# Two one-column constants in one SBUF tile: every tile allocated after them lies 32 bytes lower

## The chip, the core and the metric

The kernel runs on one core of one Trainium2 chip. The core has a matrix engine (TensorE, PE in the profile, with PEld for its weight loads), a vector engine (VectorE, DVE), a scalar engine (ScalarE, ACT), a general engine (GpSimd, POOL) and a queue that issues transfers (SyncE, SP). They share an on-chip memory, SBUF, of 128 partitions; matmul results go to a second memory, PSUM. The metric is the device time of one execution in microseconds, as the median of repeated runs.

## What is computed

The reference has two parts. The first works on `x`, 8 batches of 3008 rows by 256 features, in float32:

```
X  = rfft(x, axis=1)                       # over the 3008 rows
Yr = Xr @ w_r - Xi @ w_i + b_r
Yi = Xr @ w_i + Xi @ w_r + b_i
Yr, Yi = sign(Y) * maximum(abs(Y) - 0.01, 0)   # each of the two
y  = irfft(Yr + 1j * Yi, n=3008, axis=1)
```

The second is a feed-forward layer over all 24,064 rows of `y`, with `w_in` of 256 by 2048 and `w_out` of 2048 by 256 in float64:

```
h = y @ w_in
g = h - tanh(h)
out = g @ w_out
```

## The kernel before

**The transforms.** 3008 is 64 times 47, so a transform is done in two matrix steps, first over the 47 and then over the 64. `Forward` loads pieces of `x` (tile `xt`), splits each into a high and a low float32r part (`x_h`, `x_l`) and multiplies by the constants `f1_h`, `f1_l`; the result goes through `st` to a buffer `a` in HBM. `Spectrum` reads it back transposed (`at`), does the second step against the constant `f2`, the complex linear layer (`cross`, `shared`, line 274), the threshold, and the first inverse step (`inverse`), and stores `zo` to a buffer `z`. `Chunk.load` reads that back as `zin`.

**The feed-forward layer.** The rows are cut into 52 chunks: 50 of 470 columns and two of 282. `Chunk.time` does the last inverse step against the constant `i2` and leaves `yh`, `yl`. For each of 16 slices of the 2048 hidden units, `up` runs six matmuls into `h` (line 410), ScalarE takes the tanh (`th`, line 413), VectorE subtracts (`g`, line 415), ScalarE rounds (`gh`, line 417), VectorE takes the remainder (`gl`, line 423), and `down` runs six matmuls into the two accumulators `o` (line 435). Float64 weights are turned into `win_h`, `win_l`, `wout_h`, `wout_l` at the start by integer operations (`split_f64`).

**Order.** The order on every engine is the order in which the code is written (`manual_schedule`). The first batch goes through a path of its own (`WholeSpectrum`), before any chunk can run; the later batches' transforms are put between the feed-forward steps by a table of slots. `up` runs two steps ahead of `down`.

**Placement.** Pools take their SBUF space in the order of their tiles, each tile rounded up to a multiple of 32 bytes per partition. The pool `const` comes first, and its first tiles are the four weight tiles, 16,384 bytes each; then come `below` and `rebias`, of one float32 column each, then `f1_h` and all the rest, and after `const` the pools `load`, `work`, `cvt` and `ffn`. The slots in them are multiples of 64 bytes long; shared slots of the `ffn` pool are 2,048 bytes.

**The two constants.** `below` holds -0.01 and is the bias of the threshold's activations (lines 351 and 357). `rebias` holds -896 and is the bias of the activation that shifts the exponent in the weight conversion (line 165).

**Where a read starts.** `f2` has 384 columns; the second forward step for frequency j reads four runs of 32 columns from it, which begin `m0[j]` columns into each of its four blocks of 96 columns. `m0` comes out of `index_maps`. By its formula, the unit with j = 6 and 7 has m0 = 56 and 55, and the unit with j = 12 and 13 has m0 = 48 and 47.

Of the kernel before, what the change touches and what calls it, by code (L numbers as in the profile page):

```python
# [10 lines left out]
F32 = mybir.dt.float32  # L11
# [55 lines left out]
def spectral_ffn(ctx, tc, x, w_r, w_i, b_r, b_i, w_in, w_out, f1, f2, i1, i2, out):  # L67
    nc = tc.nc
    P = 128
# [7 lines left out]
    const = ctx.enter_context(tc.tile_pool(name="const", bufs=1))  # L77
# [410 lines left out]
    with tc.manual_schedule(engines={E.PE, E.Activation, E.DVE, E.Pool, E.SP}):  # L488
# [5 lines left out]
        def idle(n):  # L494
            ps = ps_h.tile([P, 512], F32, name="idle", tag="h")
            for _ in range(n):
                nc.tensor.matmul(ps, warm[:, :P], warm, start=True, stop=True)

        idle(11)
        below = const.tile([P, 1], F32, name="below")  # L500
        nc.vector.memset(below, -LAM)
        rebias = const.tile([P, 1], F32, name="rebias")
        nc.vector.memset(rebias, -896.0)
        f1h, f1l = split(load_whole(f1, [94, 96], "f1", tag="tmp", bufs=4), "f1")
        first = [Forward(0, ch) for ch in range(NP // XC)]
# [179 lines left out]
```

## Time and profile before

| what | value |
|---|---|
| median of 3 runs | 2722.16 us (2720.28 to 2723.64) |
| the profiled execution | 2724.98 us |
| its span from the first to the last instruction | 2723.2 us |
| mean granted TensorE clock | 0.997 |
| PE busy | 2708.1 us, 99% |
| DVE, ACT busy | 1745.8 us (64%), 1383.1 us (51%) |
| DMA queue of the kernel | 104,960 packets, 161.13 MB, 19.8% of 16 engines |

The span is what the trace covers; 1.8 us of the profiled execution's time lie outside of it. Busy time of an engine is the time in which at least one of its instructions ran. "Idle before" is the idle time of an engine just ahead of an instruction, with what ended it. Line numbers (L435) are those of the kernel before.

### The profile page before, as it was taken

Reading aid. Unit: us, or ns where it says so; the run is one execution under the profiler, and the core shown is the slowest. Engines: PE = TensorE matmul, PEld = TensorE weight load, DVE = VectorE, ACT = ScalarE, POOL = GpSimd, SP = SyncE. Lnnn points to the kernel's source line nnn. Section 1 sums busy time; section 2 is a strip of 40 time slices with the busy share of each in tenths; the row PEclk is TensorE's granted clock in tenths of the full one; section 3 lists DMA queues with packets and bytes.
Section 4 is the critical chain, followed back from the end, with each engine's and each line's share of the span. In section 5 each row is a group of like instructions: output and inputs, shape, how many; then the busy total and the mean of one; then the engine's idle time right before and its main releaser. Section 6 shows DMA issues by size and latency. Waiting matters only on the chain.

```text
span 2723.2 us, 36979 instructions
## 1 busy us (share of the span) xinstructions
PE 2708.1 (99%) x14181; PEld 2401.2 (88%) x14181; DVE 1745.8 (64%) x3077; ACT 1383.1 (51%) x2589; POOL 1.5 (0%) x5
## 2 busy tenths in 40 slices
PE   9999999999999999999999999999999999999999
PEld 6788988999889998899988999899988999888889
DVE  6796786666556666566755667666665666555555
ACT  5556455454554446454455445644455445444444
POOL 0000000000000000000000000000000000000000
PEclk8999999999999999999999999999999999999999
DMA  6413223110231103111022110411113111000000
GB/s 195 134 61 111 74 85 108 46 53 25 65 93 40 52 32 109 56 47 46 24 79 80 46 46 31 117 55 49 38 43 106 45 38 43 33 22 22 22 17 16
DMA packets 105135, 163.47 MB, mean 60 GB/s; under 512 B 7488, under 2 KB 70976, under 8 KB 104864
## 3 DMA queue, kind: packets, MB, share of 16 engines
q1 hardware_dynamic: 104960, 161.13, 19.8%
q8 instruction: 111, 1.82, 0.3%
q14 instruction: 64, 0.52, 0.1%
HBM read 86.13 MB, written 74.97 MB: 59 GB/s over the span
## 4 chain that ended last, share of the span: by engine, by line
PE 98%; DMA 1%; DVE 1%; ACT 0%; issue 0%; SPq 0%; ACTq 0%; DVEq 0%
PE o L435 38%; PE h L410 38%; PE ps_v L274 4%; PE ps_i L397 4%; PE ps_f L254 3%; PE ps_t L274 2%; PE ps_f L205 1%; PE ps_f L206 1%; PE ps_f L207 1%; PE ps_v L342 1%; PE ps_i L309 1%; PE ps_i L310 1%; PE ps_i L311 1%; DMA xt<-in_x 0%; PE ps_i L365 0%; PE ps_t L342 0%
## 5 line engine op out<-in xcount | busy, mean ns | idle before, releaser
L415 DVE TENSOR_TENSOR g<-h,th 128x470 f32<-128x470 f32 (+1 forms) x832 | 531.7, 639 | 563.1 <-ACT th L413 559.3
L413 ACT ACTIVATE th<-h 128x470 f32<-128x470 f32 (+1 forms) x832 | 463.6, 557 | 783.1 <-PE h L410 780.5
L423 DVE TENSOR_TENSOR gl<-g,gh 128x470 fp32r<-128x470 f32 (+1 forms) x832 | 531.0, 638 | 286.9 <-ACT gh L417 205.5
L417 ACT CAST gh<-g 128x470 fp32r<-128x470 f32 (+1 forms) x832 | 483.5, 581 | 403.1 <-DVE g L415 393.2
L435 PE MATMUL o<-gh,wout_l 128*128 128x470 f32 (+1 forms) x1664 | 632.1, 380 | 1.1 <-ACT gh L417 1.1
L435 PE MATMUL o<-gl,wout_h 128*128 128x470 f32 (+1 forms) x1664 | 620.1, 373 | 0.7 <-DVE gl L423 0.7
L435 PE MATMUL o<-gh,wout_h 128*128 128x470 f32 (+1 forms) x1664 | 619.8, 372 | 0.0
L410 PE MATMUL h<-yl,win_h 128*128 128x470 f32 (+1 forms) x1664 | 485.5, 373 | 0.0
L410 PE MATMUL h<-yh,win_l 128*128 128x470 f32 (+1 forms) x1664 | 484.9, 372 | 0.0
L410 PE MATMUL h<-yh,win_h 128*128 128x470 f32 (+1 forms) x1664 | 484.5, 372 | 0.0
L435 PEld LDWEIGHTS o<-gl,wout_h 128*128 128x128 f32 x1664 | 313.2, 188 | 41.2 <-DVE gl L423 1.1
L410 PEld LDWEIGHTS h<-yh,win_l 128*128 128x128 f32 x1664 | 311.5, 188 | 41.0 <-ACT yh L401 0.4
L410 PEld LDWEIGHTS h<-yl,win_h 128*128 128x128 f32 x1664 | 311.4, 188 | 40.2
L435 PEld LDWEIGHTS o<-gh,wout_l 128*128 128x128 f32 x1664 | 313.8, 189 | 37.4 <-ACT gh L417 1.6
L410 PEld LDWEIGHTS h<-yh,win_h 128*128 128x128 f32 x1664 | 311.4, 188 | 40.0
L435 PEld LDWEIGHTS o<-gh,wout_h 128*128 128x128 f32 x1664 | 313.3, 188 | 34.0
L299 DVE TENSOR_TENSOR y<-tb,ps_v 64x256 f32<-64x256 f32 x384 | 160.1, 417 | 11.9 <-ACT tb L346 6.6
L397 PEld LDWEIGHTS ps_i<-i,zin 96*128 96x128 f32 x1024 | 126.1, 192 | 4.0 <-issue 0.5
L397 PE MATMUL ps_i<-i,zin 96*128 96x94 f32 x1024 | 127.8, 272 | 0.1
L91 DVE TENSOR_TENSOR x_l<-xt,x_h 94x512 fp32r<-94x512 f32 x128 | 86.8, 686 | 50.1 <-ACT x_h L90 48.7
L254 PEld LDWEIGHTS ps_f<-f,at 128*128 128x128 f32 x768 | 101.1, 191 | 10.2 <-issue 4.4
L254 PE MATMUL ps_f<-f,at 128*128 128x128 f32 x768 | 102.6, 276 | 1.9 <-DMA at<-a 1.9
(96 smaller groups left out, 2087.4 us busy)
## 6 DMA issues: line engine op xcount, KB each, us to landing
xt<-in_x SPq DMA_DIRECT2D x64, 384.0 KB, 3.6
at<-a SPq DMA_DIRECT2D x96, 256.0 KB, 2.8
z<-zo SPq DMA_DIRECT2D x96, 256.0 KB, 2.0
out<-ot SPq DMA_DIRECT2D x50, 470.0 KB, 2.9
a<-st SPq DMA_DIRECT2D x56, 384.0 KB, 3.2
zin<-z SPq DMA_DIRECT2D x44, 480.0 KB, 4.3
w_raw<-in_moe_w_in SPq DMA_DIRECT2D x8, 512.0 KB, 5.7
w_raw<-in_moe_w_out SPq DMA_DIRECT2D x8, 512.0 KB, 4.9
```

The lines of the kernel that those rows point to most:

```text
L91: rest.tensor_tensor(out=lo, in0=src, in1=hi.bitcast(F32), op=ALU.subtract)
L205: nc.tensor.matmul(pv, f1h, xl, start=True, stop=False)
L254: nc.tensor.matmul(pv[:, t, jj], self.at[:, jj, t * P:(t + 1) * P], rhs, start=True, stop=True)
L274: nc.tensor.matmul(dst, lhs[:, t], rhs[:, t, :], start=n == 0, stop=n == 5)
L299: nc.vector.tensor_tensor(out=y[ri * 64:(ri + 1) * 64, jj, :], in0=common(jj, ri), in1=self.vv[jj * 64:(jj + 1) * 64, ri * D:(ri + 1) * D] ...
L397: nc.tensor.matmul(ps[:, k * 94:(k + 1) * 94], self.zt[:, k, t * P:(t + 1) * P], i2t[:, p * 94:(p + 1) * 94], start=True, stop=True,)
L410: nc.tensor.matmul(h[:, :n], lhs[:, t, f * P:(f + 1) * P], rhs[:, t, :n], start=k == 0, stop=k == 5)
L413: nc.scalar.activation(out=th[:, :n], in_=h[:, :n], func=AF.Tanh)
L415: nc.vector.tensor_tensor(out=g[:, :n], in0=h[:, :n], in1=th[:, :n], op=ALU.subtract)
L417: nc.scalar.copy(out=gh[:, :n], in_=g[:, :n])
L423: nc.vector.tensor_tensor(out=gl[:, :n], in0=g[:, :n], in1=gh[:, :n].bitcast(F32), op=ALU.subtract)
L435: nc.tensor.matmul(self.o[t][:, :n], lhs[:, f, t * P:(t + 1) * P], rhs[:, :n], start=f == 0 and k == 0, stop=f == NF - 1 and k == 2,)
```

## The change

One tile `shifts` of two columns takes the place of the two tiles of one column, and `below` and `rebias` become its columns 0 and 1:

```diff
         idle(11)
-        below = const.tile([P, 1], F32, name="below")
+        shifts = const.tile([P, 2], F32, name="shifts")
+        below, rebias = shifts[:, 0:1], shifts[:, 1:2]
         nc.vector.memset(below, -LAM)
-        rebias = const.tile([P, 1], F32, name="rebias")
         nc.vector.memset(rebias, -896.0)
```

The start addresses in a partition, in bytes, as the two built programs have them:

| tile | before | after |
|---|---|---|
| `win_h`, `win_l`, `wout_h`, `wout_l` | 16512, 32896, 49280, 65664 | the same |
| `below` | 82048 | 82048 |
| `rebias` | 82080 | 82052 |
| `f1_h` | 82112 | 82080 |
| `f2` | 84928 | 84896 |
| `i2` | 88000 | 87968 |
| first `xt` | 112320 | 112288 |
| first `yh` | 145088 | 145056 |
| first `gl`, `gh`, `th`, `g` | 204480, 210624, 216768, 222912 | 204448, 210592, 216736, 222880 |

Before, all tiles from `f1_h` on start at a multiple of 64 bytes (192 past a multiple of 256 for nearly all of them); after, they start 32 past a multiple of 64 (160 past a multiple of 256). The four weight tiles start at a multiple of 64 in both.

The order on VectorE at the start of the program, the difference of after from before; `zero` and `warm` feed the filler matmuls, and `f_l` is the low part of `f1`:

```order
 L490 MEMSET zero 128x512
 L492 CAST warm<-zero 128x512
-L501 MEMSET below 128x1
-L503 MEMSET rebias 128x1
+L502 MEMSET shifts 128x1
+L503 MEMSET shifts 128x1
 L91 TENSOR_TENSOR f_l<-f_f,f_h 94x96
```

The two memsets stay two and stand where they stood. On every engine and queue all instructions stand in the same order in both programs, and each waits for the same semaphore values; only addresses differ, in 16,418 of the operands that matmuls read and in nearly all operands of VectorE, ScalarE and the transfers.

## The prediction

> **What bounds the kernel now.** I read the page's head and its chain of work first, then the busy times by stage, then what TensorE waited for, then single matmuls in the timeline. These are the head, the engines' busy time and the chain:
>
> ```profile
> span 2723.2 us, 36979 instructions
> ...
> PE 2708.1 (99%) x14181; PEld 2401.2 (88%) x14181; DVE 1745.8 (64%) x3077; ACT 1383.1 (51%) x2589; POOL 1.5 (0%) x5
> ...
> PE 98%; DMA 1%; DVE 1%; ACT 0%; issue 0%; SPq 0%; ACTq 0%; DVEq 0%
> ```
>
> TensorE carries 98% of the chain. The table by stage cuts the span where the work changes: the first batch's forward step, its spectrum, the stretch with weight conversion, the steady stretch, and the end:
>
> ```profile
> 0.00:34.00 34.00, 27.81 (x94) 18.96 (x95) 17.07 (x32) 16.98 (x31) 1.49 (x5) 0.90 0.83 236
> 34.00:110.00 76.00, 72.84 (x314) 55.21 (x312) 55.09 (x116) 40.32 (x73) 0.00 (x0) 0.93 0.47 145
> 110.00:450.00 340.00, 338.20 (x1775) 297.07 (x1774) 258.51 (x459) 192.36 (x367) 0.00 (x0) 1.00 0.32 96
> 450.00:2400.00 1950.00, 1949.79 (x10301) 1741.19 (x10301) 1245.84 (x2186) 982.37 (x1834) 0.00 (x0) 1.00 0.18 54
> 2400.00:2723.20 323.20, 319.48 (x1705) 288.77 (x1703) 169.33 (x285) 151.06 (x285) 0.00 (x0) 1.00 0.06 21
> ```
>
> The columns are the stretch, its length, then busy time of PE, PEld, DVE, ACT and POOL, the granted clock, the DMA share and GB/s. From 450 to 2400 us TensorE is idle for 0.21 of 1950 us, at a full clock. So there the time is the number of matmuls by their spacing, and nothing else. Only before 110 us do other engines and transfers reach the end: PE is idle 6.19 + 3.16 us there, and the clock is at 0.90 and 0.93. What TensorE waited for at the start and in the two feed-forward products:
>
> ```profile
> PE idle L497 <- DVE rebias L503: 1.9, 1, 1.9
> ...
> PE o L435 <- ACT gh L417: 1.1, 1, 1.1
> PE o L435 <- DVE gl L423: 0.7, 1, 0.7
> ```
>
> Total, times and longest: the 9,984 matmuls of lines 410 and 435 were kept waiting twice, for 1.8 us together.
>
> **The change, part by part.** Nothing is added, removed or moved in the order: two memsets stay two, every wait stays. So each term is the price of the same instruction at another address.
>
> *The memsets and the constants.* The two memsets and their place:
>
> ```profile
> 1.80 0.06 DVE L501 MEMSET below<- 128x1 f32 x1
> 1.81 0.06 DVE L503 MEMSET rebias<- 128x1 f32 x1
> ```
>
> Each writes one column as before, 0.06 us, and the filler matmuls start behind the second as before: 0. The activations that read the constants give one comparison for free, since `below` lies at a multiple of 64 and `rebias` 32 behind one:
>
> ```profile
> L165 ACT ACTIVATE w_s<-w_s,rebias 128x512 f32<-128x512 uint32 x16 | 11.0, 716 | 1.2 <-DVE w_s L161 1.2
> L351 ACT ACTIVATE up<-y,below 128x512 f32<-128x512 f32 x12 | 8.7, 723 | 14.1 <-DVE y L299 14.1
> ```
>
> They take 716 and 723 ns for the same 512 columns. I take 0; with 16 + 12 + 11 such instructions and 7 ns between the two rows, the bound is 0.3 us either way.
>
> *TensorE's moving operands.* This is the term that could matter, since all of them but none of the feed-forward weights shift by 32 bytes. The trace of before has one place where a moving operand starts 32 bytes apart from another in the same kind of instruction: the second forward step reads `f2` from column m0[j]. Column 48 starts 192 bytes into the tile, a multiple of 64, column 56 starts at 224, 32 past one; 47 and 55 lie at 60 and 28 past one. The unit with 56 and 55, and then the one with 48 and 47, each with the start of the next matmul group:
>
> ```profile
> 1537.07 1.05 PE L254 MATMUL ps_f<-f,at 128*128 128x128 f32 x8
> 1537.88 0.46 PE L435 MATMUL o<-gh,wout_l 128*128 128x470 f32 x1
> ...
> 1596.60 1.06 PE L254 MATMUL ps_f<-f,at 128*128 128x128 f32 x8
> 1597.41 0.46 PE L435 MATMUL o<-gh,wout_l 128*128 128x470 f32 x1
> ```
>
> The first column is the start, the second the time to the last modelled end. From start to next start both take 0.81 us for eight matmuls. So 32 bytes cost at most the resolution, 0.01 us in 8, 1.3 ns each. The row has a weakness: 0.81 / 8 is 0.101 us for 128 columns, 0.79 ns per column. The feed-forward matmuls and their neighbours are quicker:
>
> ```profile
> 359.27 0.40 PE L274 MATMUL ps_v<-w_h,xl 128*128 128x256 f32 x2
> ...
> 359.51 0.40 PE L274 MATMUL ps_v<-w_l,xh 128*128 128x256 f32 x2
> ...
> 1755.15 0.39 PE L207 MATMUL ps_f<-x_h,f_h 94*96 94x512 f32 x1
> 1755.38 0.38 PE L435 MATMUL o<-gh,wout_l 128*128 128x470 f32 x1
> ...
> 1756.66 0.59 PE L410 MATMUL h<-yh,win_l 128*128 128x470 f32 x2
> ```
>
> A matmul of 256 columns takes (359.51 - 359.27) / 2 = 0.12 us, one of 512 takes 0.23 us, so a column costs 0.11 us / 256 = 0.43 ns; six of 470 columns take 1.28 us, 0.213 us each. At this pace a late fetch could show that the slower row hides. I take 0, by the row that is nearest to the case (the same engine, the same port, just these 32 bytes); the upper bound is the first rival below.
>
> [...]
>
> *VectorE and ScalarE.* All their operands move. No row of before has one of them at an address 32 bytes off the others. As the nearest bound I let every instruction lose one 64-byte piece in the 32 that 512 columns have, 3.1%. From 450 to 2400 us VectorE is idle for 1950 - 1246 = 704 us and ScalarE for 968 us, and the two waits of lines 410 and 435 above are all that they ever cost there; 39 us more of VectorE stay covered. That cover is gone only when VectorE is the bound, at over 50% more. Before 110 us the cover is thin: VectorE is busy 17.07 + 55.09 = 72.2 us and ScalarE 16.98 + 40.32 = 57.3 us, and 3.1% of both, all on the path, would be 4.0 us. I take 0, since the equal rows of TensorE and of the bias operands speak for no such piece; 0 to 4.0 us go into the range.
>
> *Transfers.* All but the weights' SBUF ends move; the HBM ends don't. These are the transfers on the chain of waits, in the first 110 us:
>
> ```profile
> 4.42 11.82 DMA xt<-in_x
> 16.30 3.31 DMA a<-st
> 28.53 2.11 DMA a<-st
> 30.79 2.69 DMA at<-a
> ...
> 102.96 1.99 DMA z<-zo
> 105.08 4.26 DMA zin<-z
> ```
>
> They hold 26.2 us of the path. One more 64-byte piece in each 2,048 bytes would make them 3.1% longer, 0.8 us; the same the other way if pieces are saved. Later transfers have the spare time of queues that are 18% and 6% busy, and TensorE's 0.21 us of idle time shows that none is late. I take 0, with 0.8 us either way.
>
> [...]
>
> **The sum.** 0 + 0 + 0 + 0 against the profiled execution's 2724.98 us, of which 1.8 us lie outside the span. That execution is 2.8 us above the median of the runs shown, 2722.16 us, which is what I forecast: 2722.2 us. The bounds of the unknown terms outside TensorE add to -1.1 and +5.1 us. A measurement of this kernel can tell about 0.2% from no change, 5.4 us.
>
> **Rivals.**
>
> *A. Slower: the fast matmuls read in 64-byte pieces.* An operand that starts 32 past a multiple then needs one piece more when its length fills its pieces. The groups concerned, with their counts:
>
> ```profile
> L205 PE MATMUL ps_f<-x_l,f_h 94*96 94x512 f32 x128 | 52.6, 411 | 2.6 <-DVE x_l L91 2.4
> L309 PE MATMUL ps_i<-z_l,i_h 128*128 128x512 f32 x84 | 33.5, 399 | 0.0
> L274 PE MATMUL ps_v<-w_h,xl 128*128 128x256 f32 x336 | 67.7, 283 | 0.0
> L274 PE MATMUL ps_t<-w_h,s_h 128*128 128x256 f32 x168 | 33.9, 283 | 0.0
> L410 PE MATMUL h<-yh,win_h 128*128 128x282 f32 x64 | 13.5, 292 | 0.0
> ```
>
> Each stands for three groups of its kind (282 columns: six, lines 410 and 435). A piece is 16 columns by 0.43 ns, 6.9 ns. 512 columns: 3 x (128 + 84) = 636, 4.4 us. 256 columns: 3 x (336 + 168) = 1512, 10.4 us. 282 columns, 1128 bytes: 18 pieces become 19, 6 x 64 = 384, 2.6 us. 470 columns are 1880 bytes and lie in 30 pieces from either start: 0. That is 17.4 us, 2739.6 us. It decides from 31% of a piece on (5.4 / 17.4). For it: nothing in before tests the fast pace. Against it: the equal pair on `f2`, where each matmul has four runs of 128 bytes that would need a third piece.
>
> *B. Faster: the moving and the weight reads get out of each other's way.* 470 columns at 0.43 ns are 202 ns, the spacing is 213: 11 ns are not columns. If they came of both reads starting at the same place of a 64-byte grid, the shift of one of the two could free some: half would be 5.5 ns by 9,600 matmuls, 53 us, 2669 us, and 0.6 ns each would already be told from noise. For it: the 11 ns, for which no wait is shown. Against it: weights are loaded while the matmul before runs, so that the two starts don't meet in time; all three buffers of `gh` and both halves of `yh` are met with one spacing.
>
> *C. Slower by the latency-bound start alone:* the bounds above, +5.1 us, 2727.3 us, with all of it on the path; that still is about no change.
>
> *D. The change doesn't do what it says:* the allocator could have kept the addresses. The two built programs show that every tile from `f1_h` on did move by 32 bytes, so this is out.
>
> **How the numbers follow.** No change, with C in it: 0.83. A above 31% of its price: 0.09. B: 0.06. Another effect of the addresses on the slower side that I have no row for: 0.02. So faster 0.06, same 0.83, slower 0.11. The range is the likeliest case's: 2722.2 with the runs' own spread of 2 us, the bounds of -1.1 and +5.1 us and as much again for another execution's level: 2716 to 2730 us. A and B lie outside; together with the rest they hold 0.17.
>
> **What would show it.** Right: line 254 still takes 0.81 us for eight, six of line 435 still 1.28 us, L274 0.12 us, L207 0.23 us; PE busy within 3 us of 2708.1; the wait rows of lines 410 and 435 stay at a few us; `rebias` in L165 stays near 716 ns. A would show as L274 at 0.127 us and L207 at 0.237 us with lines 410 and 435 at 470 columns unchanged; B as a spacing of line 435 below 0.213 us; slower vector work as a longer mean of L415 and L413 with an unchanged chain after 110 us; slower transfers as a first 110 us that ends late. The prediction is wrong if any spacing of matmuls depends on bits of the address that the two units of `f2` don't test, or if the order of memory traffic at the start settles the clock's step to full speed at another time.

## The result: 25 us faster, and the profile after

The median of four runs of the changed kernel is 2697.93 us (2694.84 to 2699.88), that of four runs of the kernel before 2722.9 us (2720.28 to 2725.59): ratio 0.9907, with a 95% interval of 0.989 to 0.9924. The forecast was no change, 2716 to 2730 us. The changed kernel's head and chain:

```profile
span 2693.1 us, 36979 instructions
...
PE 2675.0 (99%) x14181; PEld 2390.8 (89%) x14181; DVE 1746.2 (65%) x3077; ACT 1378.6 (51%) x2589; POOL 1.5 (0%) x5
...
PE 96%; DVE 2%; DMA 1%; ACT 1%; issue 0%; SPq 0%; ACTq 0%; DVEq 0%
```

The count of instructions is the same, VectorE's busy time too (1746.2 against 1745.8 us); TensorE has 33 us less busy time for the same 14,181 matmuls. By stage:

```profile
0.00:34.00 34.00, 27.60 (x110) 19.06 (x111) 18.05 (x34) 18.68 (x35) 1.49 (x5) 1.00 0.89 255
34.00:110.00 76.00, 71.95 (x344) 55.72 (x343) 58.72 (x123) 41.75 (x76) 0.00 (x0) 1.00 0.49 149
...
450.00:2400.00 1950.00, 1949.45 (x10380) 1754.23 (x10379) 1255.76 (x2201) 987.21 (x1849) 0.00 (x0) 1.00 0.18 54
```

In the steady stretch TensorE is as full as before (1949.45 of 1950 us), but 10,380 matmuls go through in place of 10,301. So they follow each other faster. Near the end of the span nothing but the feed-forward layer is left, and six matmuls of line 410 alternate with six of line 435, all of 470 columns. In the timeline three such steps lie between these rows, of the kernel before:

```profile
2500.86 0.59 PE L410 MATMUL h<-yh,win_l 128*128 128x470 f32 x2
...
2508.53 0.59 PE L410 MATMUL h<-yh,win_l 128*128 128x470 f32 x2
```

and of the kernel after:

```profile
2501.78 0.58 PE L410 MATMUL h<-yh,win_l 128*128 128x470 f32 x2
...
2509.34 0.58 PE L410 MATMUL h<-yh,win_l 128*128 128x470 f32 x2
```

36 matmuls take 7.67 us before and 7.56 us after: 0.2131 against 0.2100 us each. This accounts for the whole gain but for noise. From the starts of successive matmuls in the two traces: the spacings of line 410 at 470 columns add to 1026.7 us before and 1012.2 after, those of line 435 to 1039.8 and 1031.9, the 282-column ones to 50.4 and 49.2, line 274 to 180.4 and 179.4. That is 24.6 us. The two profiled spans differ by 30.1 us; the rest comes in the first 110 us, where the granted clock was 0.90 and 0.93 before and 1.00 after: after 408 matmuls the changed kernel is already 6.2 us ahead. That was luck of this execution. A later one of the changed kernel (run e8 below) has clocks of 0.90 and 0.93 there as well; after 408 matmuls it is 1.1 us behind the kernel before, and its span is still 23.4 us shorter, 2699.8 us.

Six undisturbed matmuls take 1.280 us before and 1.260 after, 3.3 ns less each. The gain is smaller than 9,600 x 3.3 ns = 32 us, and it is line 435 that falls short (7.9 us against 14.5 on line 410). Where a transform's matmuls break the stream, the first six behind them gain little:

```profile
1736.24 0.38 PE L435 MATMUL o<-gh,wout_l 128*128 128x470 f32 x1
...
1737.52 0.58 PE L410 MATMUL h<-yh,win_l 128*128 128x470 f32 x2
...
1738.78 0.40 PE L205 MATMUL ps_f<-x_l,f_h 94*96 94x512 f32 x1
```

Behind the three 512-column matmuls, six of line 435 take 1.28 us, the next six 1.26 us. On the mean of the traces, six of line 435 right behind line 207 went from 1.286 to 1.282 us, behind line 274 from 1.279 to 1.273 and behind line 311 from 1.279 to 1.270, in place of 0.020 less. And TensorE now reaches a few results and transfers sooner than they are ready, which costs some 1.6 us more than before:

```profile
PE o L435 <- ACT gh L417: 1.6, 1, 1.6
PE ps_i L397 <- DMA zin<-z: 1.0, 2, 0.8
PE o L435 <- DVE gl L423: 0.9, 1, 0.9
```

The other rows that the prediction named did not move. VectorE's subtraction keeps 647 ns, the conversion with `rebias` 716 ns:

```profile
L415 DVE TENSOR_TENSOR g<-h,th 128x470 f32<-128x470 f32 x800 | 517.7, 647 | 533.5 <-ACT th L413 528.5
...
L165 ACT ACTIVATE w_s<-w_s,shifts 128x512 f32<-128x512 uint32 x16 | 11.0, 716 | 1.2 <-DVE w_s L161 1.2
```

### The profile page after: what moved, and what is told of

It reads as the page before. It is cut to its first block, busy times and chain, and to the rows that moved or that the text cites. A ratio compares the mean times of both kernels' runs of the same rounds, so it can differ in the third digit from the quotient of the medians.

```text
span 2693.1 us, 36979 instructions
## 1 busy us (share of the span) xinstructions
PE 2675.0 (99%) x14181; PEld 2390.8 (89%) x14181; DVE 1746.2 (65%) x3077; ACT 1378.6 (51%) x2589; POOL 1.5 (0%) x5
## 4 chain that ended last, share of the span: by engine, by line
PE 96%; DVE 2%; DMA 1%; ACT 1%; issue 0%; SPq 0%; ACTq 0%; DVEq 0%
PE o L435 37%; PE h L410 37%; PE ps_v L274 4%; PE ps_i L397 4%; PE ps_f L254 3%; PE ps_t L274 2%; PE ps_f L205 1%; PE ps_f L207 1%; PE ps_f L206 1%; PE ps_v L342 1%; PE ps_i L310 1%; PE ps_i L311 1%; PE ps_i L309 1%; DVE g L415 1%; DMA zin<-z 0%
```

## The experiments

**First round: which relation of addresses.** Theory R was the mechanism of the prediction's rival B, moving and weight reads at the same place of a 64-byte grid; M, the moving operand's place alone; V, the other engines. The two kernels that cross the places of the weights and of all the rest:

```diff
# e1_all32, on the kernel before; e2_weights32, on the kernel after
+    const.tile([P, 8], F32, name="pad")
     win_h = const.tile([P, 2, FF], F32R, name="win_h")
```

> The kernel before with a 32-byte tile ahead of the weight tiles: the weights and all that follows start 32 past a multiple of 64. Theory R (relation): a matmul is slower when its moving operand and the weights that are being loaded start at the same place of a 64-byte grid. R expects the spacing of before, 0.213 us for 470 columns, and about 2723 us. Theory M (moving operand alone): a moving operand of 470 or 282 columns is quicker when it starts 32 past a multiple of 64. M expects 0.210 us and about 2698 us. Theory V (VectorE and ScalarE meet TensorE's weight loads): all moved together, so 2723 us as well.

> The changed kernel with a 32-byte tile ahead of the weight tiles: the weights start 32 past a multiple of 64, and all the rest is back at a multiple of 64, at the addresses of before. R expects the spacing of after, 0.210 us, and about 2698 us; M expects 0.213 us and about 2723 us.

Measured: e1 2725.13 us, ratio to before 1.0007 (0.9998 to 1.0016); e2 2698.46 us, ratio 0.9915 (0.9899 to 0.9932). Three steps of e1, then of e2, in their timelines (the lines are one further down):

```profile
2499.90 0.59 PE L411 MATMUL h<-yh,win_l 128*128 128x470 f32 x2
...
2507.58 0.59 PE L411 MATMUL h<-yh,win_l 128*128 128x470 f32 x2
```

```profile
2503.06 0.58 PE L411 MATMUL h<-yh,win_l 128*128 128x470 f32 x2
...
2510.62 0.58 PE L411 MATMUL h<-yh,win_l 128*128 128x470 f32 x2
```

7.68 / 36 = 0.2133 us and 7.56 / 36 = 0.2100 us. Everything shifted together is as slow as before; everything but the weights back at its old address, with the weights shifted, is as fast as after. M is out: it expected the opposite of both.

The third kernel shifted only the moving operands of lines 410 and 435, up by 32 bytes inside their tiles:

```diff
# e3_moving_only, on the kernel before, OFF = 8
-yh, yl: work.tile([P, 2, 512], F32R, ...)
+yh, yl: work.tile([P, 2, 512], F32R, ...)[:, :, OFF:]
-gh, gl: ffn.tile([P, CT], F32R, ...)
+gh, gl: ffn.tile([P, CT + OFF], F32R, ...)[:, OFF:]
```

> The kernel before, with yh, yl, gh and gl used from their ninth column on: the moving operands of lines 410 and 435 start 32 past a multiple of 64, every tile lies where it lay before. R and M both expect 0.210 us on these two lines and about 2698 to 2702 us. V (it was the other operands of VectorE and ScalarE) expects 0.213 us and about 2723 us.

Measured: 2725.03 us in one run, and three steps take 7.68 us, 0.2133 each:

```profile
2501.48 0.59 PE L411 MATMUL h<-yh,win_l 128*128 128x470 f32 x2
...
2509.16 0.59 PE L411 MATMUL h<-yh,win_l 128*128 128x470 f32 x2
```

So R as I had put it, a grid of 64 bytes, fell too. The fourth kernel of the round said what takes its place.

> The computation is left out: one core runs blocks of 36 equal matmuls with nothing beside them, each with its weight load, and the blocks differ in the columns and in the bytes by which the weights (w) and the moving operand (m) start past a multiple of 64. R expects 0.213 us for 470 columns where m - w is a multiple of 64 and 0.210 us where it is 32 past one, with w = 0 and w = 32 mirrored, and the same for 282 columns (0.130 against 0.127). M expects that m alone decides and w does nothing. V expects all blocks of a length alike, since no other engine runs.

In its timeline each block is one row. Letters in the names stand for digits, a for 0 to j for 9: `neha_wa_mdc` has 470 columns, the weights at 0 and the moving operand 32 bytes past the tile's start. Both tiles start at the same place modulo 256. The time of a block runs to the next row's start:

```profile
17.37 7.84 PE L45 MATMUL neha_wa_ma<-moving,weight 128*128 128x470 f32 x36
25.05 7.84 PE L45 MATMUL neha_wa_me<-moving,weight 128*128 128x470 f32 x36
...
55.64 7.73 PE L45 MATMUL neha_wa_mdc<-moving,weight 128*128 128x470 f32 x36
63.21 7.87 PE L45 MATMUL neha_wa_mea<-moving,weight 128*128 128x470 f32 x36
...
132.24 7.95 PE L45 MATMUL neha_wa_mbjc<-moving,weight 128*128 128x470 f32 x36
140.03 7.84 PE L45 MATMUL neha_wa_mcce<-moving,weight 128*128 128x470 f32 x36
...
193.92 7.87 PE L45 MATMUL neha_wdc_mdc<-moving,weight 128*128 128x470 f32 x36
201.62 7.78 PE L45 MATMUL neha_wdc_mea<-moving,weight 128*128 128x470 f32 x36
...
224.53 7.73 PE L45 MATMUL neha_wdc_mge<-moving,weight 128*128 128x470 f32 x36
232.10 7.84 PE L45 MATMUL neha_wdc_mia<-moving,weight 128*128 128x470 f32 x36
...
403.07 7.96 PE L45 MATMUL neha_wge_ma<-moving,weight 128*128 128x470 f32 x36
410.87 7.87 PE L45 MATMUL neha_wjg_ma<-moving,weight 128*128 128x470 f32 x36
```

With the weights at 0, the moving operand at 0 takes 7.68 us for 36 (0.2133), at 32 takes 7.57 (0.2103), at 192 takes 7.79 (0.2164). With the weights at 32, the moving operand at 32 takes 7.70 and at 64 takes 7.57. So the distance d, moving start minus weight start, decides, with no other engine running: V is out. But the value at d = 96 is 0.2136, not fast, so it is not a grid of 64. And with the weights at 64 the moving operand at 0, d = -64, takes 7.80 us, as d = 192 does: the spacing goes by d modulo 256. That is R256. It is not exact for every start: with the weights at 48 the moving operand at 0 (d = 208) took 7.76 us, where the later blocks, with the weights at 0, have 7.68 at this distance. R256 explains the round: before, the moving operands start 192 past a multiple of 256 and the weights 128, d = 64 (0.2134 in the blocks); after, 160 - 128 = 32 (0.2100); e1, 224 - 160 = 64; e2, 192 - 160 = 32; e3, 224 - 128 = 96 (0.2136).

**Second round: R256 tested on the kernel.** The edit is that of e3 with other shifts, so that d takes two values that the blocks had as fast and slow, and one kernel has it on `gh` and `gl` alone.

> The kernel before, with yh, yl, gh and gl used from their fifth column on: only the moving operands of lines 410 and 435 shift, by 16 bytes up, so that d goes from 64 to 80; all tiles lie where they lay. R256 expects 0.210 us for 470 columns and, as after, about 2699 us. Theory M (moving operand 32 past a multiple of 64) and theory V (other engines' operands) both expect 0.213 us and about 2723 us.

> The same with a shift of 128 bytes, d = 192. R256 expects the slow value of the grid, 0.217 us, and a kernel slower than before by about what after gained: 2745 to 2755 us. M and V expect 0.213 us and 2723 us.

> As with d = 80, but for gh and gl alone: line 435 at d = 80, line 410 at d = 64. R256 expects 0.210 us on line 435 and 0.213 us on line 410, and half of the gain, about 2711 us. If the spacing came of any of the two lines' other operands, both lines would change or none.

Measured: e4 2702.71 us, ratio 0.9924 (0.9907 to 0.9941); e5 2743.0 us, 1.0074 (1.0054 to 1.0094); e6 2713.3 us, 0.9961 (0.9948 to 0.9974). A step of e4:

```profile
2504.43 0.58 PE L411 MATMUL h<-yh,win_l 128*128 128x470 f32 x2
...
2506.95 0.58 PE L411 MATMUL h<-yh,win_l 128*128 128x470 f32 x2
```

three steps of e5:

```profile
2502.06 0.59 PE L411 MATMUL h<-yh,win_l 128*128 128x470 f32 x2
...
2509.86 0.59 PE L411 MATMUL h<-yh,win_l 128*128 128x470 f32 x2
```

and six matmuls of line 410, then six of line 435, of e6:

```profile
2501.27 0.58 PE L411 MATMUL h<-yh,win_l 128*128 128x470 f32 x2
...
2502.54 0.37 PE L436 MATMUL o<-gh,wout_l 128*128 128x470 f32 x1
...
2503.80 0.58 PE L411 MATMUL h<-yh,win_l 128*128 128x470 f32 x2
```

e4 has 2.52 / 12 = 0.2100 us, e5 7.80 / 36 = 0.2167 us, each the blocks' value. A shift of 16 bytes does most of what the change did, 20 us of 25 (line 410 has 0.2111 us on the mean of its trace, so not every stretch reaches 0.2100), and one of 128 bytes makes the kernel slower than before. e5's time came short of the 2745 us expected, as the gain of after does, and for the same reason: its line 435 has 0.2152 us on the mean of the spacings below 250 ns. In e6 line 435 takes 1.26 / 6 = 0.2100 and line 410 1.27 / 6 = 0.2117 here. On the whole trace the spacings of line 435 add to 9.3 us less than before and those of line 410, which the expectation had unchanged, to 3.7 us less: about half of the gain, mostly on the line that was shifted.

The blocks of the same round went through all distances:

> The computation is left out: blocks of 36 equal matmuls with nothing beside them, for distances d = moving start minus weight start (in bytes, modulo 256) in steps of 4 for 470 columns, in steps of 16 for 512 and 256 columns, and with 96, 64 and 32 weight columns. [...] The rival F (a fixed cost per matmul beside the dependence on d): with 32 weight columns still over 0.208 us.

For 470 columns the spacing runs from 0.210 us (at d = 32, 76, 80, 108, 176 and 236) to 0.219 or 0.220 us (at 60, 120 and 180), and is 0.213 at most others; I see no simple order in it. The row of d = 80, and the blocks with 32 weight columns (`cdc`, at d = 0, 32, 64, 192):

```profile
170.17 7.72 PE L44 MATMUL cbci_neha_dia<-moving,weight 128*128 128x470 f32 x36
177.74 7.84 PE L44 MATMUL cbci_neha_die<-moving,weight 128*128 128x470 f32 x36
...
771.91 7.99 PE L44 MATMUL cdc_neha_da<-moving,weight 128*32 128x470 f32 x36
779.74 7.90 PE L44 MATMUL cdc_neha_ddc<-moving,weight 128*32 128x470 f32 x36
787.48 7.79 PE L44 MATMUL cdc_neha_dge<-moving,weight 128*32 128x470 f32 x36
795.11 7.77 PE L44 MATMUL cdc_neha_dbjc<-moving,weight 128*32 128x470 f32 x36
```

Here R256 missed twice. If the weight load took turns with the moving reads, fewer weight columns would shorten the spacing and take the dependence on d away. A quarter of the weight columns leaves 7.83, 7.74 and 7.63 us for 36 at d = 0, 32 and 64, that is 0.2175, 0.2150 and 0.2119 us, where 128 columns have 7.68, 7.57 and 7.69 us, though the weight load itself takes 109 ns in these blocks and 188 with 128 columns. So the part of the spacing that is not columns does not follow the length of the weight load, as the rival F had it. And the dependence on d did not go away; it changed: d = 32 is no longer a fast distance, d = 64 is faster.

**Third round: whose weights, which operands, and a version with more.**

> The computation is left out: blocks of 72 matmuls of 470 columns that alternate between two pairs of weights and moving operand. In one block each matmul is at a fast distance (32) from its own weights and at a slow one (0 and 64) from the weights of the matmul behind it; in the next the reverse; then two blocks with both fast and both slow. If the distance to the next matmul's weights decides, which are loaded while this one streams, the first block takes 0.213 us and the second 0.210 us each; if the distance to its own weights decides, the other way round. Both fast: 0.210; both slow: 0.213.

```profile
23.66 15.52 PE L48 MATMUL own_fast_next_slow<-moving,weight 128*128 128x470 f32 x72
39.02 15.41 PE L48 MATMUL own_slow_next_fast<-moving,weight 128*128 128x470 f32 x72
54.27 15.29 PE L48 MATMUL both_fast<-moving,weight 128*128 128x470 f32 x72
69.40 15.53 PE L48 MATMUL both_slow<-moving,weight 128*128 128x470 f32 x72
84.77 15.53 PE L48 MATMUL warm<-moving,weight 128*128 128x470 f32 x72
```

From start to start, for 72: 15.36, 15.25, 15.13 and 15.37 us, that is 0.2133, 0.2118, 0.2101 and 0.2135. A fast distance to its own weights alone gains nothing, one to the next matmul's weights alone gains half of the way, and the whole way needs both. So the next weights, which are loaded while a matmul streams, have a part in it by themselves, and not all of it as the expectation had it; why its own count as well is open.

> The computation is left out: blocks of 36 equal matmuls of 470 columns in bfloat16 at twelve distances, and of 416, 448, 480 and 496 columns in float32r at d = 0, 32, 64 and 192. If the dependence on the distance belongs to operands of four bytes, all bfloat16 blocks take the same time, shorter than 0.210 us; if it is one of any two reads beside each other, they differ as the float32r blocks do. For float32r the distance is expected to matter at each number of columns, by up to 7 ns, with the same sign at 32 for none of them in particular.

Two of the bfloat16 blocks, then the weight loads of all of them and of one float32r block (busy time in us and mean ns of one, behind the bar):

```profile
15.94 7.32 PE L49 MATMUL bf_neha_da<-moving_b,weight_b 128*128 128x470 bf16 x36
23.09 7.30 PE L49 MATMUL bf_neha_dbg<-moving_b,weight_b 128*128 128x470 bf16 x36
...
L49 PEld LDWEIGHTS <-weight_b 128*128 128x128 bf16 x432 | 42.2, 98 | 43.5 <-issue 0.3
L49 PEld LDWEIGHTS fr_nejg_dge<-moving,weight 128*128 128x128 f32 x36 | 6.8, 188 | 1.4
```

In bfloat16 the eleven blocks from d = 0 to d = 224 take 7.14 or 7.15 us each, 0.1983 us a matmul, and the spacings inside the twelfth, d = 240, are the same. So the dependence on the distance, and 12 to 22 ns of each matmul with it, come with float32r. Whether the four bytes of the operands are the reason is not shown: the weight load differs as well, 98 ns in bfloat16 against 188 in float32r. In float32r the other numbers of columns differ by distance too: 448 columns from 0.200 us at d = 64 to 0.207 at d = 0, 416 from 0.187 to 0.189.

Last, the linear layer's weights, the moving operands of line 274, were put 192 bytes further, since blocks of 256 columns took 0.120 us at d = 0 and 0.114 at 192, and the changed kernel was run again beside it:

```diff
# e7_linear_d192, on the kernel after
+            if i in (0, 3):
+                const.tile([P, 48 if i == 0 else 16], F32, name=f"pad{i}")
             if i < 3:
                 lin.append(split(whole_lin[i], f"w{i + 1}"))
```

> The changed kernel with the linear layer's weights w1 to w3 in a place 192 bytes further (modulo 256), so that the moving operand of line 274 goes from d = 0 to d = 192, and lines 410 and 435 stay at d = 32. Theory R256 with the grid of 256 columns (0.120 us at d = 0, 0.113 at 192) expects 1512 x 6 ns = 9 us less than after, about 2689 us. If the grid doesn't hold there, because the matmuls of line 274 are mixed with others, about 2698 us.

> The changed kernel once more, on the same chip as the version above, to compare the two: about 2698 us by every theory.

Measured: e7 2694.56 us, ratio to before 0.9893 (0.9878 to 0.9908); e8 2699.49 us, 0.9907 (0.9891 to 0.9924). By its median the version is the fastest of all, but not for the reason given. Two matmuls of line 274 in e7:

```profile
1529.35 0.40 PE L274 MATMUL ps_v<-w_h,xl 128*128 128x256 f32 x2
1529.59 0.40 PE L274 MATMUL ps_v<-w_l,xh 128*128 128x256 f32 x2
```

still take 0.24 us; on the mean of the trace 118.0 ns against 118.7 in e8, 1.0 us in all. The blocks' value did not carry over to line 274. Line 435 went from 211.3 to 210.8 ns on the mean of spacings below 250 ns, 2.6 us, and most of it on the matmuls right behind line 274: six of them take 1.262 us in e7 and 1.273 in e8, in 189 places. So the shift paid on the matmuls that follow, which no theory here had; why is open. The rest of the 4.9 us is within a run's spread of 4 us.

## Why the prediction was wrong, by its steps

*What bounds the kernel* held: TensorE's spacing is the time, and the change reached the time through it: 24.6 us of spacings for 25 us of time.

*The memsets, the constants, VectorE, ScalarE* held at 0: 647 and 716 ns are unchanged, and e4 gets 0.9924 with all of their tiles in place. *Transfers* held within what can be told: with the clock of before in the first 110 us (e8), the first 408 matmuls took 1.1 us longer than before, where the term had been given 0.8 us either way. The 64-byte pieces behind the bounds of 4.0 us (VectorE, ScalarE) and 0.8 us (transfers) were my assumption; no run shows them.

*TensorE's moving operands* is the step that failed. It took 0 from two units of line 254 that lie 32 bytes apart and take the same 0.81 us. That row was near in bytes and far in kind: a float32 matmul at 0.79 ns per column, not a float32r one at 0.43. I had written that a faster pace could show what it hides, and then let it stand as the value all the same. What the runs showed in its place: -3.3 ns on each undisturbed matmul of 470 columns, -24.6 us over the lines that changed.

In the kernel the shift of the moving operands down by 32 bytes, with the feed-forward weights in place, took the spacing from 0.2131 to 0.2100 us. With nothing else running, the place of the moving operand relative to the weights changes the float32r spacing by up to 10 ns (m2: 0.2100 us at d = 76, 0.2200 at d = 120), and the next weights' place alone by 1.7 ns (m3: 0.2135 to 0.2118 us). In bfloat16 the distance changes nothing: 0.1983 us at all twelve (m4).

*Rival A* is out: line 274 did not get slower (180.4 against 179.4 us), and a moving operand that starts 32 past a multiple of 64 is not slower in itself. In the blocks, 36 matmuls of 512 columns take 8.20 us with both operands at 0 and 8.19 with both at 32, but 8.41 with the moving operand alone at 32. On the lines that A named the weights moved along with the operands, except for the 282 columns, which got faster (50.4 to 49.2 us).

*Rival B* named the engine, the two reads and the sign, at a chance of 0.06 and a price of 53 us. Three of its points were wrong. Its grid of 64 bytes was one of 256, with more values than two (0.210 to 0.220 us in m2). Its objection, that the starts of the two reads don't meet in time, does not matter: the distance modulo 256 does, in a pattern that has to be measured. And its size, half of the 11 ns, was a guess: 3.3 of the 11 ns went on undisturbed matmuls, 24.6 us in all in place of 53. Its evidence against, one spacing for all buffers, was no evidence: all of them lay at the same place modulo 256, so on these lines the trace of before had no variation in the one quantity that counts. The chance for no change was taken from that silence.

## What to carry to other kernels

In a kernel whose matmuls read float32r operands back to back, each with its own weight load, the place of the moving tiles relative to the weight tiles, modulo 256 bytes, can matter: in the blocks of m2 it was worth up to 5% of a matmul (0.210 to 0.220 us for 470 columns), and in this kernel one merged constant moved it from 64 to 32. So compare the spacing of matmuls, not only their order, after an edit that only adds or merges a constant. A few blocks of bare matmuls find the good distances for the shapes of a kernel in one run; a value found so must still be tried in the kernel (it held for lines 410 and 435, not for 274). And a row that shows equal times counts as evidence only at the pace of the instructions in question.

## What was not expected of the hardware

Float32r matmuls of 470 columns that follow each other settle to a spacing of 213.3 ns at d = 64 and 210.0 at d = 32, with VectorE and ScalarE busy beside them or not: the blocks with no other engine running have 213.5 and 210.1 ns (m3). Behind the matmuls of line 274, of another shape, the stream of the changed kernel needs four to five matmuls to reach 210 ns: the spacings there are 216, 212, 213, 213, 211 and 209 ns on the mean. And the 12 to 22 ns by which float32r stays above bfloat16's 198.3 ns remain with a quarter of the weight columns, so where they come from is open.
